# A 32-head attention with a gated GLU: the last two head groups alternate by chunk, output projections spread over the last blocks, |q| by a bit mask

## The chip, the cores and the metric

One core of a Trainium2 chip. Its engines work side by side, each on its own in-order stream of instructions: TensorE (PE, matmuls; the loads of its stationary operand are listed as PEld), VectorE (DVE), ScalarE (ACT), GpSimd (POOL) and SyncE (SP), which issues nearly all of the DMAs. The metric is the device time of one execution in microseconds; the median of the runs counts. A profile is one execution recorded by the hardware; its span runs from the first to the last instruction.

## The reference

With S = 2048 rows, D = 640, 32 heads of 20 channels and F = 1728:

```python
xn = layernorm(x)                                     # (2048, 640)
q, k, v = heads(xn @ wqkv)                            # 32 heads, Dh = 20
p = softmax(q @ k.T * Dh ** -0.5)                     # 2048 x 2048 for each head
s = concat_heads(p @ v) @ wo
g = silu((sigmoid(xn @ w_gate) * (xn @ w_up)) @ w_down)
out = x + s * g
```

All inputs and the output are bfloat16.

## The kernel before

**Blocks.** The heads are taken in 8 groups of 4 (`NG`, `GH`), the queries in 4 chunks of 512 (`NQC`, `QC`). A block is one group with one chunk, `g, c = divmod(b, NQC)`: 32 blocks, all four chunks of a group behind one another. A block has 4 x 16 score tiles of 128 keys x 512 queries. The four heads of a group lie 32 partitions apart, so that their small matmuls run beside each other in PE. The keys of a group are in `kTs[g % 2]`, the queries of a block in `qts[b % 3]`.

**Exponentials.** They are shared between two engines. ACT takes tiles in slots of two or three: two banks `scA[0]`/`scA[1]` of 128x1024, and at times one of the three spare banks `bank` (`bk` in the profile), with `exp_act` (L80). DVE takes the others from a `bk` bank: one conversion to int16 (`iv`, L1194) and, for four tiles at once, three passes (L945, L948, L951) that make two bfloat16 factors, which PE sums up; so a DVE tile costs two attention matmuls. The attention matmuls (L897) add into one bank, `oacc`, whose row 0 of each head is the sum of the exponentials.

**The quotient.** At a block's end `norm_a` copies `oacc` to `on` (L910) and sends the sums through DRAM (`ld`, `lt`); `norm_b` takes the reciprocal (`rt`), sends it through DRAM again (`rd`, `rl`), multiplies on POOL (`on_bf`, L927) and stores the heads' rows into `oU` (L935), the transposed input of the output projection, four or five DMAs for a block. For block 30, the last but one, another way is taken: `mk_div` transposes `on` on PE, divides on DVE, transposes back and keeps the group's 80 rows in `oL`; the projection of chunk 2 has a sixth matmul with `oL` and `wo_l`, the last 80 rows of `wo`. Block 31 takes the same way in the steps `e_on` (L985), `e_tr` (L989), `e_scale`, `e_back` (L998), `e_o` (L1002).

**The work around it.** Beside scores and attention, PE has items, each a list of operations on several engines in one spare bank: keys, queries and values of the next groups; for each chunk the GLU's gate and up (`mk_gu`, L641) and down (`mk_down`, L679; its `td` on ACT, `gqs` on DVE, then a store to `gq_dram`); and the output projection `mk_out` of a row tile `tt` and a half `h` of the columns. `mk_qu` makes the queries of 6 heads: an evacuation to `qu`, and |q| of it (L547), for a bound on the scores.

`mk_out(tt, h)` has five matmuls of 320 columns (L765), a `scalar_tensor_tensor` on DVE with the GLU result (`otmp`, L772), an addition of x on POOL or DVE (L775), and after the second half the store of the tile (L777). `load_out` brings x and the GLU result of the tile into one of three slots that lie over `xnT` (L743, L744); a slot is taken again by tile `tt + 3`.

**Tail.** The last chunk's four tiles are not made by `mk_out`. `fill` holds 40 early matmuls (L976): for each tile 5 of 512 and 5 of 128 columns over the rows of `oU` that the first seven groups fill. Those that the planner finds no gap for are put out at the start of `tail_steps`. Four plus four late matmuls (L980) add the last group, then come the evacuations (L1020 to L1032) and the stores (L1036). Their x and GLU rows are loaded by `tail_load` (L964, L965) into space of `wd`, the weights of the down projection, once no GLU item is left.

**Order.** PE, ACT and DVE run in an order written out by a planner in the kernel: a loop over a clock of its own, with a fixed cost for each operation, that decides at each step which engine takes what. PE fills an ACT slot when it is free and otherwise goes on with attention matmuls or an item. `items` have an earliest block (`at`), conditions (`pre`) and, for projections, a block whose quotient must be done (`need`); an item that may run goes ahead of the GLU's. `due()` says how much of the item work should be done by now; `M_END` is how many blocks before the end all of it should be. `can_fill` lets early matmuls in when all scores are claimed and PE has nothing else. SP and POOL are not planned: their streams follow the order in which buffers come free.

Of the kernel before, what the change touches and what calls it, by code (L numbers as in the profile page):

```python
# [10 lines left out]
FP32 = mybir.dt.float32  # L11
# [19 lines left out]
URGENT, ROUNDS, HOLD, SLACK, LEAD, LAG, D_LAST, D_LAST_END = 0.25, 4, 0.15, 0.2, 40.0, 0.0, 20, 8  # L31
D_ORD, M_ORD, WAIT3, FALL, M_END = 1, 0, 0.4, 1, 1.5
NPT, NPB, NIV = (3, 7), 3, 3
# [16 lines left out]
def kernel(  # L50
# [375 lines left out]

    NBLK = NG * NQC
    NJOB = GH * TT
    q_at = {0: 0.0}
# [109 lines left out]
    def mk_qu(u, c, at):  # L539
        st = {}  # L540

        def alloc():
            st["ps"] = misc_ps()

        def ab():
            aqs[(u, c)] = wk.tile([P, QC], BF16, tag="aq", bufs=4, name="aq")
            nc.vector.scalar_tensor_tensor(out=aqs[(u, c)][0:UC, :], in0=st["q"], scalar=-1.0, in1=st["q"],  # L547
                                           op0=ALU.mult, op1=ALU.max)

        def ev():  # L550
            st["q"] = wk.tile([P, QC], BF16, tag="ku", bufs=2, name="qu")[0:UC, :]
            nc.vector.tensor_scalar_mul(out=st["q"], in0=st["ps"][0:UC, :], scalar1=qscale)
            nc.sync.dma_start(out=qD[u][:, c * QC:(c + 1) * QC], in_=st["q"])
        return Item([("PE", alloc, [(T_MM, lambda kd=kd: u_mm(st, u, 0, c, kd)) for kd in range(KD)]),
                     ("DVE", 0.60, ev, "free", mark("qD", u, c)),
                     ("DVE", 0.60, ab, "", mark("aq", u, c))], at, pre=[("bD", u - 1)] if u else [])

# [38 lines left out]
    def load_q(b):  # L596
        g, c = divmod(b, NQC)
# [100 lines left out]
    wo_l = late.tile([GC, D], BF16, name="wo_l")  # L698
    oL = []

    def div_scale(tps):
# [6 lines left out]
        return onq  # L708

    def mk_div(on, b):  # L710
        st = {}

        def a1():
            st["t"] = misc_ps()

        def a2():
            st["u"] = misc_ps().bitcast(BF16)

        def tr(i):
            nc.tensor.transpose(out=st["t"][:, i * P:(i + 1) * P], in_=on[:, i * P:(i + 1) * P], identity=ident_f)  # L720

        def sc():
            st["q"] = div_scale(st["t"])

        def back():
            for i in range(4):
                nc.tensor.transpose(out=st["u"][0:GC, i * P:(i + 1) * P], in_=st["q"][:, i, :], identity=ident)

        def ev():
            o = w2.tile([GC, QC], BF16, tag="on_bf", bufs=2, name="oL")  # L730
            nc.vector.tensor_copy(out=o, in_=st["u"][0:GC, 0:QC])
            oL.append(o)
        return [Item([("PE", a1, [(0.22, lambda i=i: tr(i)) for i in range(4)]),
                      ("DVE", 0.75, sc, "free", mark("div", b))], 0.0, pre=[("on", b)]),
                Item([("PE", a2, [(0.30, back)]),
                      ("DVE", 0.40, ev, "free", lambda t: o_at.__setitem__(b, t))], 0.0, pre=[("div", b)])]

# [8 lines left out]
    def mk_out(tt, h, at):  # L746
        st = {}

        def alloc():
            if h == 0:  # L750
                load_out(tt)
                if (tt + 1) % 4:
                    load_out(tt + 1)
            st["ps"] = misc_ps()

        split = tt // 4 == NQC - 2

        def mm(kd):
            hs = slice(h * HD, (h + 1) * HD)
            if kd == KD:  # L760
                lhsT, rhs = oL[0][:, tt % 4 * P:(tt % 4 + 1) * P], wo_l[:, hs]
            else:
                rows = o_l if split and kd == t_l else P
                lhsT, rhs = oU[0:rows, kd, tt * P:(tt + 1) * P], wo[0:rows, kd, hs]
            nc.tensor.matmul(st["ps"][:, 0:HD], lhsT=lhsT, rhs=rhs, start=(kd == 0),  # L765
                             stop=(kd == KD - 1 + split))

        def ev():
            xr, gqr = out_tiles[tt]
            sl = slice(h * HD, (h + 1) * HD)  # L770
            tmp = w2.tile([P, HD], FP32, tag="gqs", bufs=3, name="otmp")
            nc.vector.scalar_tensor_tensor(out=tmp, in0=st["ps"][:, 0:HD], scalar=0.25,  # L772
                                           in1=gqr[:, sl], op0=ALU.mult, op1=ALU.mult)
            add = nc.vector if h == 1 and claimed[0] == NJOB * NBLK else nc.gpsimd
            add.tensor_tensor(out=xr[:, sl], in0=tmp, in1=xr[:, sl], op=ALU.add)  # L775
            if h == 1:
                nc.sync.dma_start(out=out2[tt * P:(tt + 1) * P, :], in_=xr)  # L777
        return Item([("PE", alloc, [(0.136, lambda kd=kd: mm(kd)) for kd in range(KD + split)]),
                     ("DVE", 0.40, ev, "free", mark("o", tt, h))], at, need=(NG - 1) * NQC + tt // 4,
                    pre=[("d", tt // 4, t4, i) for t4 in range(4) for i in range(2)] + [("h", 2, kf) for kf in range(NFT)] + (  # L780
                        [("o", tt - 2, 1)] if h == 0 and tt > 1 else []))
# [12 lines left out]
    for b in range(NBLK):  # L794
        g, c = divmod(b, NQC)
        mk = []
# [62 lines left out]
    def score_mm(dst, b, kt, j):  # L859
        nc.tensor.matmul(dst, lhsT=kTs[(b // NQC) % 2][32 * j:32 * j + 32, kt * P:(kt + 1) * P],  # L860
                         rhs=qts[b % 3][32 * j:32 * j + 32, :], start=True, stop=True, tile_position=(32 * j, 0))
# [16 lines left out]
    def pv_pick(j):  # L878
        for u in pv_q[j]:
            if u["b"] == pv_block[0] and u["ready"] <= now and v_at.get((u["b"] // NQC // 2, u["kt"]), 1e9) <= now:  # L880
                return u
        return None
# [4 lines left out]
    def pv_emit(us, end):  # L887
        for u in us:
            b, kt, j, k = u["b"], u["kt"], u["j"], u["k"]
            pr, go = divmod(b // NQC, 2)  # L890
            pv_q[j].remove(u)
# [25 lines left out]
    def norm_b(b, on, lt):  # L917
        g, c = divmod(b, NQC)
        rt = w2.tile([P, GH * QC // P], FP32, tag="rt", bufs=2, name="rt")
# [90 lines left out]
    def tail_steps():  # L1010
        for _, _, f in fill:
            f()
        for t4 in range(4):
# [24 lines left out]
    with tc.manual_schedule(engines={ENG.PE, ENG.Activation, ENG.DVE}):  # L1038
# [59 lines left out]
        chain_at = 1e9  # L1098
        while chain or items or glu_items or any(it.i < len(it.ops) for it in active):
            guard += 1  # L1100
            assert guard < 120000, "the issue order does not end"
            bb = base()
            if bb > blk_loaded:
                blk_loaded = bb
                g, c = divmod(bb, NQC)
                if c == 0 and g + 1 < PG:
# [18 lines left out]
            if q_next < NBLK and base() >= q_next - 2:  # L1125
                us_ = [u for u, _, _, _ in spans(q_next // NQC)]
                if all(ev_at.get(("qD", u, q_next % NQC), 1e9) <= now and ev_at.get(("bD", u), 1e9) <= now for u in us_) \
                        and q_next // NQC in k_at:
                    load_q(q_next)
                    q_at[q_next] = max(now + 5.0, k_at[q_next // NQC])  # L1130
                    q_next += 1

            for eng in ("ACT", "DVE"):
# [99 lines left out]
            if free["PE"] <= now:  # L1233
# [45 lines left out]
                if nxt == "F":  # L1279
# [111 lines left out]
```

## Time and profile before

| | us |
|---|---|
| runs (3) | 840.9, 841.19, 842.89 |
| median | 841.19 |
| profiled execution, span | 839.8 |
| mean granted TensorE clock | 0.997 |

A row of groups reads: line, engine, operation, out<-in, shapes, xcount | busy us, mean ns of one | idle time before them, and what ended it. A row of the timeline: start, length, engine, line, operation, xcount, and in brackets the idle time before it. A row of windows: stretch, its length, the busy time of each engine with its count of instructions, the granted clock, the share of the DMA engines, GB/s. The profile's line numbers are those of the kernel before.

### The profile page before, as it was taken

What the parts mean: (1) busy time and instruction counts of PE and PEld (TensorE: products, weight loads), DVE (VectorE), ACT (ScalarE), POOL (GpSimd) and SP (SyncE); (2) the same over time, 40 slices, a digit from 0 to 9 for tenths busy, and PEclk for the clock granted to TensorE, in tenths of its full rate; (3) what the DMA queues carried; (4) which work ended last, traced back from release to release, by engine and by line L of the source; (5) the groups of instructions that cost most, each with busy time, mean ns of one, the idle gap of its engine ahead of it and who ended that gap; (6) DMA issues with size and microseconds to landing.
All of it is one profiled execution on the core that took longest, in us unless ns stands there. A gap on an engine that the chain in (4) does not pass through costs nothing.

```text
span 839.8 us, 16932 instructions
## 1 busy us (share of the span) xinstructions
PE 788.4 (94%) x6354; PEld 278.5 (33%) x6411; DVE 765.4 (91%) x1194; ACT 796.0 (95%) x1003; POOL 77.5 (9%) x84
## 2 busy tenths in 40 slices
PE   4799999999999999999999999999999999999995
PEld 2432323333333323333333233333233322333342
DVE  7789899999899998998999999999998988999994
ACT  7799999999999999999999999999999999999970
POOL 5000000000000001000000000000000000002333
PEclk9999999999999999999999999999999999999998
DMA  5711212123222132213121232131311223111642
GB/s 154 205 51 50 60 51 49 47 57 82 72 62 63 43 85 69 68 44 82 52 61 53 68 85 67 45 92 49 109 65 46 66 71 78 28 47 57 193 147 91
DMA packets 92979, 62.21 MB, mean 74 GB/s; under 512 B 34648, under 2 KB 86408, under 8 KB 92896
## 3 DMA queue, kind: packets, MB, share of 16 engines
q1 hardware_dynamic: 92608, 60.79, 25.7%
q8 instruction: 50, 0.82, 0.4%
q10 hardware_dynamic: 288, 0.33, 0.1%
q14 instruction: 33, 0.27, 0.1%
HBM read 46.24 MB, written 12.39 MB: 70 GB/s over the span
## 4 chain that ended last, share of the span: by engine, by line
ACT 49%; PE 28%; DVE 13%; issue 6%; DMA 2%; SPq 1%; POOL 0%; POOLq 0%; ACTq 0%; DVEq 0%
ACT pt L80 44%; PE scA L860 8%; PE oacc L897 5%; DVE iv L1194 5%; PE bk L679 4%; PE bk L641 3%; ACT tnh L80 3%; DVE pb L951 2%; PE bk L765 2%; PE bk L504 2%; DVE pb L945 1%; DVE pb L948 1%; DMA ld<-on 1%; PE psk L140 1%; ACT td L80 1%
## 5 line engine op out<-in xcount | busy, mean ns | idle before, releaser
L80 ACT ACTIVATE pt<-scA 128x1024 bf16<-128x1024 f32 (+1 forms) x729 | 720.2, 1153 | 4.6 <-PE bk L860 2.9
L1194 DVE TENSOR_SCALAR iv<-bk 128x512 int16<-128x512 f32 x471 | 318.6, 682 | 31.7 <-PE bk L860 30.2
L860 PE MATMUL scA<-q,kT 32*128 32x512 bf16 x1448 | 282.6, 382 | 16.7 <-ACT pt L80 9.6
L860 PE MATMUL bk<-q,kT 32*128 32x512 bf16 x600 | 215.5, 383 | 2.0 <-DVE iv L1194 1.7
L897 PE MATMUL oacc<-pt,v 128*21 128x512 bf16 x1577 | 183.1, 382 | 0.6 <-ACT pt L80 0.3
L860 PEld LDWEIGHTS <-kT 32*128 32x128 bf16 x2048 | 88.7, 91 | 261.6 <-issue 246.8
L897 PE MATMUL oacc<-pb,v 128*21 128x512 bf16 x942 | 152.9, 382 | 1.8 <-DVE on L910 1.5
L951 DVE TENSOR_TENSOR pb<-iv,pb 128x2048 bf16<-128x2048 bf16 x118 | 146.8, 1244 | 0.8
L641 PE MATMUL bk<-xnT,wgu 128*128 128x512 bf16 x471 | 142.6, 383 | 3.6 <-issue 1.7
L927 POOL TENSOR_TENSOR on_bf<-on,rl 128x512 bf16<-128x512 f32 x30 | 43.3, 1443 | 692.7 <-DMA rl<-rd 326.0
L80 ACT ACTIVATE pt<-bk 128x512 bf16<-128x512 f32 x129 | 94.5, 733 | 4.0 <-PE bk L860 3.8
L945 DVE TENSOR_SCALAR pb<-iv 128x2048 int16<-128x2048 int16 x118 | 86.3, 731 | 2.5
L679 PE MATMUL bk<-wd,hT 128*128 128x320 bf16 x448 | 86.9, 302 | 1.2 <-DVE iv L1194 0.7
L948 DVE TENSOR_SCALAR pb<-iv 128x2048 int16<-128x2048 int16 x118 | 82.6, 700 | 0.0
L897 PEld LDWEIGHTS <-v 128*21 128x21 bf16 x2519 | 50.4, 90 | 92.2 <-issue 69.4
L641 PEld LDWEIGHTS <-wgu 128*128 128x128 bf16 x520 | 37.1, 97 | 66.2 <-issue 50.4
L679 PEld LDWEIGHTS <-hT 128*128 128x128 bf16 x448 | 34.4, 97 | 48.4 <-issue 39.4
L504 PE MATMUL bk<-xnT,wu 128*120 128x512 bf16 x160 | 49.3, 399 | 0.4 <-DVE iv L1194 0.3
L80 ACT ACTIVATE tnh<-bk 128x512 bf16<-128x512 f32 (+1 forms) x56 | 41.6, 742 | 0.1
L649 DVE SCALAR_TENSOR_TENSOR hT<-tnh,bk 128x512 bf16<-128x512 bf16 x52 | 35.3, 680 | 5.9 <-PE bk L641 5.2
L612 PE MATMUL bk<-wv,xnT 128*128 128x160 bf16 x280 | 29.2, 234 | 0.7 <-ACT pt L80 0.6
L612 PEld LDWEIGHTS <-xnT 128*128 128x128 bf16 x280 | 18.6, 98 | 14.4 <-issue 14.1
(116 smaller groups left out, 381.3 us busy)
## 6 DMA issues: line engine op xcount, KB each, us to landing
wgu<-in_B_w_gate_dram SPq DMA_DIRECT2D x24, 320.0 KB
wgu<-in_B_w_up_dram SPq DMA_DIRECT2D x24, 320.0 KB
rl<-rd SPq DMA_DIRECT2D x120, 64.0 KB
gq_dram<-gqs SPq DMA_DIRECT2D x32, 160.0 KB
xnT<-gq_dram SPq DMA_DIRECT2D x12, 320.0 KB
xt<-in_A_x_dram SPq DMA_DIRECT2D x16, 160.0 KB
wd<-in_B_w_down_dram SPq DMA_DIRECT2D x1, 2080.0 KB
oU<-on_bf SPq DMA_DIRECT2D x104, 20.0 KB
```

What stands on the lines that cost most here:

```text
L80: return nc.scalar.add_instruction(mybir.InstActivation(func=func, name=nc.get_next_instruction_name(), engine=ENG.Activation, ins=[nc.sca ...
L504: nc.tensor.matmul(st["ps"][0:UC, :], lhsT=wus[u][:, kd, i, :], rhs=xnT[:, c, kd, :], start=(kd == 0), stop=(kd == KD - 1))
L612: nc.tensor.matmul(st["ps"][:, i * 2 * GC:(i + 1) * 2 * GC], lhsT=xn_tok(tts[i], kd), rhs=wvs[pr][:, kd, :], start=(kd == 0), stop=(kd == ...
L641: nc.tensor.matmul(st[key][0:fs, :], lhsT=w[:, i, kd, ko * P:ko * P + fs], rhs=xnT[:, c, kd, :], start=(kd == 0), stop=(kd == KD - 1))
L679: nc.tensor.matmul(st["ps"][:, 0:HD], lhsT=hT[0:fsz[kf], kf, t4 * P:(t4 + 1) * P], rhs=wd[0:fsz[kf], kf, h * HD:(h + 1) * HD], start=(kf = ...
L860: nc.tensor.matmul(dst, lhsT=kTs[(b // NQC) % 2][32 * j:32 * j + 32, kt * P:(kt + 1) * P], rhs=qts[b % 3][32 * j:32 * j + 32, :], start=Tr ...
L897: nc.tensor.matmul(oacc[32 * j:32 * j + DH + 1, :], lhsT=lhsT, rhs=u["src"], start=first, stop=last, tile_position=(0, 32 * j), skip_group ...
L927: nc.gpsimd.tensor_tensor(out=on_bf, in0=on, in1=rl, op=ALU.mult)
L945: nc.vector.tensor_scalar(out=pb[:, 0, :, :].bitcast(I16), in0=iv, scalar1=0x7F80, scalar2=1, op0=ALU.bitwise_and, op1=ALU.bitwise_or)
L948: nc.vector.tensor_scalar(out=pb[:, 1, :, :].bitcast(I16), in0=iv, scalar1=0x007F, scalar2=0x3F00, op0=ALU.bitwise_and, op1=ALU.bitwise_or)
L951: nc.vector.tensor_tensor(out=pb[:, 1, :, :], in0=iv.bitcast(BF16), in1=pb[:, 1, :, :], op=ALU.mult)
L1194: nc.vector.tensor_scalar(out=d["iv"][:, j, :], in0=bank[bk], scalar1=B_OFF, scalar2=0.0, op0=ALU.add, op1=ALU.max)
```

## The change

1. From block 24 (`ALT`) on, groups 6 and 7 alternate: block 24 is group 6 chunk 0, block 25 group 7 chunk 0, block 26 group 6 chunk 1, and so on. The keys of both groups stay in their two buffers. A chunk's attention is complete after blocks 25, 27, 29 and 31, where before it was after 28, 29, 30 and 31.
2. The projections are listed four halves to a block from block 26 on, with `need` at the chunk's own last block.
3. Block 30 takes the quotient's common way; `mk_div`, `oL` and the sixth matmul are gone. Block 30 is now group 6, chunk 3.
4. The early matmuls that were left to `tail_steps` are all given out in the planner's loop, which goes on until they are.
5. |q| is made by clearing the sign bit of the bfloat16 value as an int16, planned at 0.19 in place of 0.60 us.
6. `M_END` goes from 1.5 to 2.25 blocks.

```diff
-D_ORD, M_ORD, WAIT3, FALL, M_END = 1, 0, 0.4, 1, 1.5
+D_ORD, M_ORD, WAIT3, FALL, M_END = 1, 0, 0.4, 1, 2.25
...
+    ALT = (NG - 2) * NQC
+
+    def gc_of(b):
+        if b < ALT:
+            return divmod(b, NQC)
+        return NG - 2 + (b - ALT) % 2, (b - ALT) // 2
...
-            nc.vector.scalar_tensor_tensor(out=aqs[(u, c)][0:UC, :], in0=st["q"], scalar=-1.0, in1=st["q"],
-                                           op0=ALU.mult, op1=ALU.max)
+            nc.vector.tensor_scalar(out=aqs[(u, c)][0:UC, :].bitcast(I16), in0=st["q"].bitcast(I16), scalar1=0x7FFF,
+                                    scalar2=0, op0=ALU.bitwise_and, op1=ALU.bitwise_or)
...
-                     ("DVE", 0.60, ab, "", mark("aq", u, c))], at, pre=[("bD", u - 1)] if u else [])
+                     ("DVE", 0.19, ab, "", mark("aq", u, c))], at, pre=[("bD", u - 1)] if u else [])
...
-    def mk_div(on, b):
...
-        split = tt // 4 == NQC - 2
-
         def mm(kd):
             hs = slice(h * HD, (h + 1) * HD)
-            if kd == KD:
-                lhsT, rhs = oL[0][:, tt % 4 * P:(tt % 4 + 1) * P], wo_l[:, hs]
-            else:
-                rows = o_l if split and kd == t_l else P
-                lhsT, rhs = oU[0:rows, kd, tt * P:(tt + 1) * P], wo[0:rows, kd, hs]
-            nc.tensor.matmul(st["ps"][:, 0:HD], lhsT=lhsT, rhs=rhs, start=(kd == 0),
-                             stop=(kd == KD - 1 + split))
+            nc.tensor.matmul(st["ps"][:, 0:HD], lhsT=oU[:, kd, tt * P:(tt + 1) * P], rhs=wo[:, kd, hs],
+                             start=(kd == 0), stop=(kd == KD - 1))
...
-        return Item([("PE", alloc, [(0.136, lambda kd=kd: mm(kd)) for kd in range(KD + split)]),
-                     ("DVE", 0.40, ev, "free", mark("o", tt, h))], at, need=(NG - 1) * NQC + tt // 4,
+        return Item([("PE", alloc, [(0.136, lambda kd=kd: mm(kd)) for kd in range(KD)]),
+                     ("DVE", 0.40, ev, "free", mark("o", tt, h))], at, need=ALT + 1 + 2 * (tt // 4),
...
-        if b >= NBLK - NQC and c > 0:
-            for t4 in range(4):
-                for h in range(2):
-                    mk.append(lambda at, t=4 * (c - 1) + t4, h=h: [mk_out(t, h, at)])
+        if b >= ALT + 2:
+            n = (b - ALT - 2) * 4
+            for i in range(n, n + 4):
+                mk.append(lambda at, t=i // 2, h=i % 2: [mk_out(t, h, at)])
...
     def tail_steps():
-        for _, _, f in fill:
-            f()
...
-        while chain or items or glu_items or any(it.i < len(it.ops) for it in active):
+        while chain or fill or items or glu_items or any(it.i < len(it.ops) for it in active):
...
-                    if norm_pending[0] == NBLK - 2:
-                        on = w2.tile([P, QC], FP32, tag="on", bufs=2, name="on")
-                        nc.vector.tensor_copy(out=on, in_=oacc)
-                        items[0:0] = mk_div(on, norm_pending[0])
-                        ev_at[("on", norm_pending[0])] = free["DVE"] + EL
-                    else:
-                        timed.append((free["DVE"] + 6.5, norm_pending[0]) + norm_a(norm_pending[0]))
+                    timed.append((free["DVE"] + 6.5, norm_pending[0]) + norm_a(norm_pending[0]))
...
-                    elif m_ok:
-                        nxt = "M"
+                    else:
+                        nxt = "M" if m_ok else None
```

Elsewhere `divmod(b, NQC)` and `b // NQC` become `gc_of(b)`, in the loads of keys and queries, the scores, the values and the quotient.

More of the change, by code (lines that the diff above doesn't have):

```diff
@@ L596, in load_q @@
     def load_q(b):
-        g, c = divmod(b, NQC)
+        g, c = gc_of(b)
         cs = slice(c * QC, (c + 1) * QC)
@@ L698 @@
     wo_l = late.tile([GC, D], BF16, name="wo_l")
-    oL = []
     def div_scale(tps):
@@ L708, in div_scale @@
         return onq
-    def mk_div(on, b):
[L711 to L736, printed above, removed]
     def load_out(tt):
@@ L794 @@
     for b in range(NBLK):
-        g, c = divmod(b, NQC)
+        g, c = gc_of(b)
         mk = []
@@ L859, in score_mm @@
     def score_mm(dst, b, kt, j):
-        nc.tensor.matmul(dst, lhsT=kTs[(b // NQC) % 2][32 * j:32 * j + 32, kt * P:(kt + 1) * P],
+        nc.tensor.matmul(dst, lhsT=kTs[gc_of(b)[0] % 2][32 * j:32 * j + 32, kt * P:(kt + 1) * P],
                          rhs=qts[b % 3][32 * j:32 * j + 32, :], start=True, stop=True, tile_position=(32 * j, 0))
@@ L879, in pv_pick @@
         for u in pv_q[j]:
-            if u["b"] == pv_block[0] and u["ready"] <= now and v_at.get((u["b"] // NQC // 2, u["kt"]), 1e9) <= now:
+            if u["b"] == pv_block[0] and u["ready"] <= now and v_at.get((gc_of(u["b"])[0] // 2, u["kt"]), 1e9) <= now:
                 return u
@@ L889, in pv_emit @@
             b, kt, j, k = u["b"], u["kt"], u["j"], u["k"]
-            pr, go = divmod(b // NQC, 2)
+            pr, go = divmod(gc_of(b)[0], 2)
             pv_q[j].remove(u)
@@ L917, in norm_b @@
     def norm_b(b, on, lt):
-        g, c = divmod(b, NQC)
+        g, c = gc_of(b)
         rt = w2.tile([P, GH * QC // P], FP32, tag="rt", bufs=2, name="rt")
@@ L1104 @@
                 blk_loaded = bb
-                g, c = divmod(bb, NQC)
+                g, c = gc_of(bb)
                 if c == 0 and g + 1 < PG:
@@ L1125 @@
             if q_next < NBLK and base() >= q_next - 2:
-                us_ = [u for u, _, _, _ in spans(q_next // NQC)]
-                if all(ev_at.get(("qD", u, q_next % NQC), 1e9) <= now and ev_at.get(("bD", u), 1e9) <= now for u in us_) \
-                        and q_next // NQC in k_at:
+                us_ = [u for u, _, _, _ in spans(gc_of(q_next)[0])]
+                if all(ev_at.get(("qD", u, gc_of(q_next)[1]), 1e9) <= now and ev_at.get(("bD", u), 1e9) <= now for u in us_) \
+                        and gc_of(q_next)[0] in k_at:
                     load_q(q_next)
-                    q_at[q_next] = max(now + 5.0, k_at[q_next // NQC])
+                    q_at[q_next] = max(now + 5.0, k_at[gc_of(q_next)[0]])
                     q_next += 1
```

## The prediction

> **What bounds the kernel now.** I read the page's engine totals and slices first, then the busy time by stage, then the end of the run in order of time.
>
> ```profile
> span 839.8 us, 16932 instructions
> PE 788.4 (94%) x6354; PEld 278.5 (33%) x6411; DVE 765.4 (91%) x1194; ACT 796.0 (95%) x1003; POOL 77.5 (9%) x84
> PE   4799999999999999999999999999999999999995
> ACT  7799999999999999999999999999999999999970
> ```
>
> ScalarE (ACT) is full from the third slice to the last but one, and then empty while TensorE (PE) goes on. The stages, with the busy time of each engine:
>
> ```profile
> core 0: us, PE busy (x) PEld busy (x) DVE busy (x) ACT busy (x) POOL busy (x), PEclk, DMA share, GB/s
> 60.00:812.70 752.70, 727.06 (x5889) 249.04 (x5939) 705.23 (x1074) 746.51 (x921) 56.22 (x45) 1.00 0.24 68
> 777.00:787.00 10.00, 9.84 (x84) 3.58 (x82) 9.93 (x17) 10.00 (x12) 4.79 (x6) 1.00 0.52 160
> 812.70:823.00 10.30, 10.28 (x67) 5.14 (x65) 8.14 (x17) 0.00 (x0) 2.67 (x4) 1.00 0.55 175
> 823.00:830.30 7.30, 7.27 (x44) 3.10 (x44) 1.07 (x3) 0.00 (x0) 1.41 (x2) 1.00 0.20 67
> 830.30:839.80 9.50, 0.87 (x5) 0.20 (x2) 4.94 (x7) 0.00 (x0) 3.82 (x3) 0.73 0.20 71
> ```
>
> From 60 us to 812.7 ACT is idle for 752.70 - 746.51 = 6.2 us, VectorE (DVE) for 47.5, PE for 25.6: the exponentials set the pace. From 812.7 on ACT has nothing; PE is the bound for 17.6 us, and the last 9.5 us are the final evacuations and stores. So the time is the end of the last exponential, E, plus a tail.
>
> ```profile
> 799.64 6.53 ACT L80 ACTIVATE pt<-scA 128x1024 bf16<-128x1024 f32 x7
> 805.97 0.70 ACT L80 ACTIVATE pt<-bk 128x512 bf16<-128x512 f32 x1
> 806.45 2.06 ACT L80 ACTIVATE pt<-scA 128x1024 bf16<-128x1024 f32 x2
> 808.73 3.96 ACT L80 ACTIVATE pt<-scA 128x1024 bf16<-128x1024 f32 x4
> ```
>
> E = 808.73 + 3.96 = 812.69, and the tail is 839.8 - 812.69 = 27.1 us. From start to start a 128x1024 exponential costs (805.97 - 799.64) / 7 = 0.904 us and a 128x512 one 806.45 - 805.97 = 0.48; the longer means below overlap.
>
> **The change, part by part.** The issue orders of the two built programs (they hold no times) give the counts.
>
> *Exponentials.* The planner hands six score tiles more to ACT: 728 exponentials of 128x1024 in place of 719, 127 of 128x512 in place of 139 (129 + 10 below).
>
> ```profile
> L80 ACT ACTIVATE pt<-scA 128x1024 bf16<-128x1024 f32 x719 | 715.3, 1160 | 4.6 <-PE bk L860 2.9 <-PE scA L860 1.0
> L80 ACT ACTIVATE pt<-bk 128x512 bf16<-128x512 f32 x129 | 94.5, 733 | 4.0 <-PE bk L860 3.8
> L80 ACT ACTIVATE td<-bk 128x320 bf16<-128x320 f32 x32 | 17.3, 541 | 0.0
> L80 ACT ACTIVATE pt<-scA 128x512 bf16<-128x512 f32 x10 | 7.1, 708 | 0.0
> ```
>
> That is 9 x 0.904 - 12 x 0.48 = +2.4 us on the engine that sets the pace. One `td` now stands behind the last exponential; it takes about 0.4 us out from in front of E. If ACT's idle time stays as it is, E' = 812.69 + 2.4 - 0.4 = 814.7. The idle time is the unknown: at best its 6.2 us vanish, at worst I allow as much again.
>
> *Bit mask.* Sixteen instructions of 703 ns change form. No bitwise row has 512 elements; those of 1536 and 2048 carried on in a straight line give 551 - 2 x 150 = 251 ns and 546 - 2 x 187 = 172 ns, and 551 is an upper bound. I take 0.21.
>
> ```profile
> L945 DVE TENSOR_SCALAR pb<-iv 128x2048 int16<-128x2048 int16 x117 | 85.8, 733 | 2.5
> L948 DVE TENSOR_SCALAR pb<-iv 128x2048 int16<-128x2048 int16 x117 | 82.0, 701 | 0.0
> L547 DVE SCALAR_TENSOR_TENSOR aq<-qu 120x512 bf16<-120x512 bf16 x16 | 11.3, 703 | 0.0
> L948 DVE TENSOR_SCALAR pb<-iv 128x1536 int16<-128x1536 int16 x1 | 0.6, 551 | 0.0
> L945 DVE TENSOR_SCALAR pb<-iv 128x1536 int16<-128x1536 int16 x1 | 0.5, 546 | 0.0
> ```
>
> DVE is freed of 16 x 0.49 = 7.9 us (2.4 at the upper bound). On the path this is worth nothing: DVE already has 47.5 us idle beside a full ACT, and the score tiles move the other way. It would count only if DVE's lateness made ACT's 6.2 us of idle time.
>
> *Projections out of the tail.* Before, some 50 output matmuls stand on PE after E. After, all 120 stand ahead of the last score, and the eight with `oL` are gone with the two transposes of `mk_div`. Five `wd` matmuls and the 40 early matmuls remain after the last score. Prices:
>
> ```profile
> 808.29 0.84 PE L765 MATMUL bk<-wo,oU 128*128 128x320 bf16 x5 [0.23 <-DVE iv L1194]
> 814.72 0.68 DVE L985 COPY on<-oacc 128x512 f32<-128x512 f32 x1
> 815.46 0.66 PE L989 MATMUL scA<-ident_f,on 128*128 128x128 f32 x4
> 817.46 0.39 PE L998 MATMUL tp<-ident,onq 128*80 128x128 bf16 x4
> 823.03 2.42 PE L976 MATMUL scA<-wo,oU 128*128 128x512 bf16 x9
> 825.38 4.60 PE L976 MATMUL bk<-wo,oU 128*128 128x512 bf16 x30
> 830.34 0.69 DVE L1020 SCALAR_TENSOR_TENSOR hT<-bk,wd 128x512 f32<-128x512 f32 x1 [5.02 <-PE bk L980]
> ```
>
> 50 x 0.84 / 5 = 8.4 us of PE work goes under ACT, where PE has 25.6 us idle; I cost it at nothing, and at up to 8.4 us if that room is not usable. The added quotient chain of block 30 (one POOL multiplication, five kinds of DMA) lies beside the last block.
>
> Tail before: 2.0 us from E to the copy of `oacc` (814.72), 15.6 us to the first evacuation (830.34), 9.5 us to the end. The last stays. Of the twenty 512-wide early matmuls (0.245 us each: ten in 2.42), seven now stand between the last attention matmuls, thirteen behind the copy, then the twenty 128-wide ones (4.60 less ten at 0.25, so 2.1 us). From the copy to the first evacuation: 13 x 0.245 + 0.66 + 0.39 + 2.1, and 0.36 for the late ones (825.38 + 4.60 to 830.34), = 6.7 us. From E' to the copy I take 2.9 instead of 2.0, since four of the seven stand ahead of the last attention matmul. PE is then ready at E' + 9.6.
>
> *What is late next.* Two transfers. The early matmuls read block 30's `oU`, where before block 27's was the last they needed; and the reload of the GLU result for the tail, hidden before, now begins when the last `wd` matmul has run, because it overwrites `wd`.
>
> ```profile
> 770.93 0.68 DVE L910 COPY on<-oacc 128x512 f32<-128x512 f32 x1
> ```
>
> ```profile
> 785.91 3.04 SPq L935 DMA_DIRECT2D oU<-on_bf  x4
> 789.05 0.42 SPq L777 DMA_DIRECT2D out_dram<-xnT  x1
> 789.52 0.92 SPq L964 DMA_DIRECT2D wd<-in_A_x_dram  x1
> 794.33 0.38 SPq L691 DMA_DIRECT2D gq_dram<-gqs  x1
> 799.90 0.32 SPq L965 DMA_DIRECT2D wd<-gq_dram  x1
> ```
>
> Copy to last `oU` issue was 788.95 - 770.93 = 18.0 us; with a fifth `oU` transfer (0.76) and about 2 us to land, 21. Block 30's copy stands 18 score fills before the end: 18 x 0.904 + 5 x 0.48 + some 1.1 = 19.8 us before E'. So `oU` lands near E' + 1.2; the matmul that reads it is due at E' + 1.4 to 1.7. It just fits, within about 2 us either way.
>
> Before, nine loads (five of 160 KB, four of 320) and the store at 794.33 (160 KB) took from 789.52 until 799.90, when the load that waits for that store went out: 2240 KB in 10.4 us. SP's queue is in order, so after, the first load goes out at about E' + 0.2, behind block 30's `oU` and tile 11's store; six loads (1440 KB) stand before the last store (160 KB). 1600 / 2240 x 10.4 = 7.4 us, so the last reload goes out at E' + 7.6 and lands some 2.9 later (2.4 as in the row among the rivals, and the doubled size): E' + 10.5. That is later than PE's E' + 9.6, so the transfer decides, by 0.9.
>
> The Trainium skill, "DMA: Bandwidth & Descriptors", section Bandwidth, measures 341 GB/s for 1 MB, which as an estimate moves 1600 KB in 4.8 us; PE would decide then and the sum would be 0.9 lower. The row is of the same loads in the same company, and I keep it.
>
> Sum: 814.7 + 10.5 + 9.5 = 834.7 us of span. The profiled execution's span is 839.8 and the runs' median 841.19; with the same 1.4 us around it, **836 us**.
>
> **Rivals.**
> - *The tail's transfers are later still* (0.13). For it: no matmul waited for these `oU` rows before, and the quotient chain now shares SP's queue with the stores of tiles 8 to 10, each waiting for its POOL addition. Against: both were priced with company. 3.5 us more: 839.5.
> - *PE has no room* (0.10). The 8.4 us come back, less what ACT absorbs, as a later E: about 842, no change. For it: only 25.6 us of 752.7 idle. Against: from 800 to E projections ran beside exponentials standing start to start. The Trainium skill, "Trace Analysis", section Identifying the Most-Contended Engine, says that matmul busy time is a bad measure of PE's headroom and weight-load time a better one; here that is 249.04 of 752.7. By the page there is ample room and this rival would be worth 0.05; the sum is the same by both.
> - *Slower: the tiles' turnover holds DVE* (0.08). Three slots in `xnT` serve twelve tiles. A slot takes its next row of x only when the last store has landed, and DVE's in-order `otmp` stands before the int16 conversions whose banks PE needs:
>
> ```profile
> 778.39 2.39 DMA out_dram<-xnT
> 780.80 2.20 DMA xnT<-in_A_x_dram
> ```
>
> Two such pieces in a row are 4.6 us, against some 1.8 us of exponentials queued ahead. It decides from 0.65 us lost per tile (7.8 in twelve); at 1 us each, 848. Against: while this very chain ran, ACT was busy 10.00 of 10.00 us (777 to 787), and the tiles are now spread over five blocks in place of three.
> - *DVE was the hidden bound* (0.05): the mask's 7.9 us let ACT's idle time nearly vanish: 831.
>
> **How the numbers follow.** The forecast has 0.64, spread over 832 to 838.7 by the idle time (about 3 either way) and the transfers (about 2). The range from 831 to 843.5 leaves out the slower rival and the ends of the others, some 0.14. Counting as equal what lies within 0.3% of 841.19 (838.7 to 843.7): faster 0.72 (forecast 0.62, hidden bound 0.05, late tail 0.05), same 0.16, slower 0.12.
>
> **What would show it.** Right: the last exponential ends at 813 to 817; no output projection after it; the copy of `oacc` 2.5 to 3.5 us later; the first evacuation some 10.5 us after E', waiting for a transfer of `wd<-gq_dram` rather than for PE; the bit mask near 0.2 us, and DVE idler than before. Wrong: E' beyond 820 with ACT idle in front of score matmuls, PE waiting for `oU` before its early matmuls for over 3 us, or `otmp` waiting for transfers in the last eight blocks.

## The result and the profile after

| | before | after |
|---|---|---|
| median, us | 841.4 (4 runs, 840.9 to 842.89) | 837.4 (4 runs, 835.54 to 838.14) |
| ratio of the times, 95% interval | | 0.9947 [0.9932, 0.9961] |
| profiled execution: time, span | span 839.8 | 838.14, span 836.4 |
| end of the last exponential, E | 812.69 | 816.77 |
| E to the copy of `oacc` | 2.0 | 3.05 |
| E to the first evacuation | 17.65 | 10.64 |
| E to the end (tail) | 27.1 | 19.6 |

The change makes the kernel faster by 0.5%. The page of after, its first lines and two rows of its slices:

```profile
span 836.4 us, 16903 instructions
PE 782.4 (94%) x6330; PEld 276.5 (33%) x6389; DVE 751.7 (90%) x1178; ACT 798.5 (95%) x1000; POOL 83.2 (10%) x90
PE   4899999999999999999999999999999999999995
ACT  7699999999999999999999999999999999999990
```

The totals of PE and ACT hardly move, DVE's falls by 13.7 us. ACT's last busy slice is fuller (9 in place of 7), and the whole run ends earlier. The end of ACT's stream in after, from its timeline:

```profile
815.20 0.66 ACT L80 ACTIVATE pt<-bk 128x512 bf16<-128x512 f32 x1
815.67 1.10 ACT L80 ACTIVATE pt<-scA 128x1024 bf16<-128x1024 f32 x1
816.58 0.53 ACT L80 ACTIVATE td<-bk 128x320 bf16<-128x320 f32 x1
```

E' (the E of after) = 815.67 + 1.10 = 816.77, 4.1 us later than before. After it stands one `td`, as the issue order said. The tail of after, in the timelines of PE and DVE:

```profile
817.37 0.59 PE L946 MATMUL scA<-wo,oU 128*128 128x512 bf16 x2 [0.16 <-issue]
818.22 1.25 PE L946 MATMUL scA<-wo,oU 128*128 128x512 bf16 x4
819.40 0.39 PE L867 MATMUL oacc<-pb,v 128*21 128x512 bf16 x1
822.96 2.87 PE L946 MATMUL bk<-wo,oU 128*128 128x512 bf16 x23
825.76 0.40 PE L950 MATMUL bk<-wo_l,o 80*128 80x128 bf16 x4
```

```profile
819.82 0.69 DVE L955 COPY on<-oacc 128x512 f32<-128x512 f32 x1 [1.79 <-PE oacc L867]
827.41 0.69 DVE L988 SCALAR_TENSOR_TENSOR hT<-bk,wd 128x512 f32<-128x512 f32 x1 [3.77 <-DMA wd<-gq_dram]
```

No output projection (L735) stands behind E'. The 0.16 us before the first early matmul are no wait for block 30's `oU`: the same 0.16 us stand there with M_END 1.5 (below), where the early matmuls begin 7.5 us after E. So no wait for the quotient's transfers shows; by how much they were in time isn't shown. PE is ready for the first evacuation at 825.76 + 0.40, which is E' + 9.4. The reload of the last GLU tile comes last: DVE, idle for 3.77 us, goes on 1.25 us after PE is ready. The chain of waits of after and SP's queue:

```profile
820.11 4.44 DMA gq_dram<-gqs
...
824.62 2.72 DMA wd<-gq_dram
...
827.41 0.70 DVE hT L988
```

```profile
816.89 0.37 SPq L934 DMA_DIRECT2D wd<-in_A_x_dram  x1
...
820.11 0.33 SPq L697 DMA_DIRECT2D gq_dram<-gqs  x1
820.54 0.98 SPq L934 DMA_DIRECT2D wd<-in_A_x_dram  x1
824.62 0.32 SPq L935 DMA_DIRECT2D wd<-gq_dram  x1
```

The loads begin 0.1 us after E', the store stands behind six of them, and the reload goes out when the store has landed, 824.62 - 816.89 = 7.7 us after the first load (7.4 forecast).

Half of the reason why E' is late lies in the head of the run. Two stretches of after, then the same of before; the columns are stretch and length, busy time of PE, PEld, DVE, ACT, POOL, the granted clock, the DMA share and GB/s:

```profile
31.00:35.00 4.00, 1.53 (x10) 0.33 (x9) 3.01 (x7) 1.21 (x4) 0.00 (x0) 0.80 1.13 315
35.00:40.50 5.50, 5.49 (x38) 3.43 (x38) 2.35 (x4) 4.32 (x5) 0.00 (x0) 0.52 1.07 362
```

```profile
31.00:35.00 4.00, 1.81 (x18) 0.99 (x19) 3.02 (x7) 1.46 (x3) 0.00 (x0) 1.00 1.13 308
35.00:40.50 5.50, 4.96 (x52) 2.71 (x51) 4.29 (x7) 5.50 (x8) 0.00 (x0) 1.00 1.08 350
```

In both, PE has just waited 1.30 and 0.79 us for DVE. In the profile of after the granted clock then goes to 0.52, PE is full and yet feeds ACT 4.32 us of work in place of 5.50. Over the first 60 us ACT is busy 47.47 us in after and 49.48 in before: 2.0 us, half of E's delay. This is not the change. The kernel with doubled output matmuls, below, has after's issue order there and keeps 1.00; the run with the mask alone has the order of before and falls to 0.50. Their second stretches, in this order:

```profile
35.00:40.50 5.50, 5.03 (x53) 2.70 (x53) 4.46 (x8) 5.50 (x7) 0.00 (x0) 1.00 1.08 350
35.00:40.50 5.50, 5.50 (x35) 3.04 (x33) 3.33 (x6) 4.53 (x6) 0.00 (x0) 0.50 1.09 344
```

The fastest of the four runs of after, 835.54 us, had a mean clock of 0.996; the others took 836.98 to 838.14 us at 0.990 to 0.992. The other half of E's delay is work, the longer list of exponentials: from 60 us to E' ACT is idle for 756.77 - 750.69 = 6.1 us, as before (6.2).

```profile
60.00:816.77 756.77, 729.08 (x5928) 250.37 (x5980) 699.54 (x1072) 750.69 (x920) 66.19 (x55) 1.00 0.25 68
```

### The profile page after: what moved, and what is told of

Its sections match the earlier page's. It is cut to its first block, busy times and chain, and to the rows that moved or that the text cites. A ratio compares the mean times of both kernels' runs of the same rounds, so it can differ in the third digit from the quotient of the medians.

```text
span 836.4 us, 16903 instructions
## 1 busy us (share of the span) xinstructions
PE 782.4 (94%) x6330; PEld 276.5 (33%) x6389; DVE 751.7 (90%) x1178; ACT 798.5 (95%) x1000; POOL 83.2 (10%) x90
## 4 chain that ended last, share of the span: by engine, by line
ACT 49%; PE 29%; DVE 11%; issue 7%; DMA 2%; SPq 1%; POOLq 0%; POOL 0%; ACTq 0%; DVEq 0%
ACT pt L80 45%; PE scA L830 9%; PE oacc L867 6%; PE bk L685 4%; DVE iv L1156 4%; PE bk L647 4%; ACT tnh L80 2%; DVE pb L921 2%; PE bk L510 2%; DVE pb L915 1%; DVE pb L918 1%; PE bk L735 1%; PE bk L618 1%; PE psk L140 1%; DMA lt<-ld 1%
## 5 line engine op out<-in xcount | busy, mean ns | idle before, releaser
L80 ACT ACTIVATE pt<-scA 128x1024 bf16<-128x1024 f32 x734 | 722.1, 1147 | 5.7 <-PE bk L830 1.9
L830 PE MATMUL scA<-q,kT 32*128 32x512 bf16 x1462 | 285.8, 384 | 17.9 <-ACT pt L80 10.5
L830 PE MATMUL bk<-q,kT 32*128 32x512 bf16 x586 | 211.7, 386 | 1.4 <-DVE iv L1156 1.2
L867 PE MATMUL oacc<-pb,v 128*21 128x512 bf16 x930 | 150.6, 382 | 1.0 <-DVE pb L915 0.4
L921 DVE TENSOR_TENSOR pb<-iv,pb 128x2048 bf16<-128x2048 bf16 (+1 forms) x117 | 145.6, 1245 | 0.7
L80 ACT ACTIVATE pt<-bk 128x512 bf16<-128x512 f32 x121 | 86.7, 717 | 4.2 <-DVE oacc L388 2.8
L915 DVE TENSOR_SCALAR pb<-iv 128x2048 int16<-128x2048 int16 (+1 forms) x117 | 84.5, 722 | 2.7
L918 DVE TENSOR_SCALAR pb<-iv 128x2048 int16<-128x2048 int16 (+1 forms) x117 | 83.4, 713 | 0.0
L618 PE MATMUL bk<-wv,xnT 128*128 128x160 bf16 x280 | 31.6, 243 | 1.1 <-DVE v L189 0.5
L745 POOL TENSOR_TENSOR xnT<-otmp,xnT 128x320 bf16<-128x320 f32 x24 | 24.2, 1011 | 45.7 <-DVE otmp L742 45.5
```

The lines of the kernel that those rows point to most:

```text
L80: return nc.scalar.add_instruction(mybir.InstActivation(func=func, name=nc.get_next_instruction_name(), engine=ENG.Activation, ins=[nc.sca ...
L618: nc.tensor.matmul(st["ps"][:, i * 2 * GC:(i + 1) * 2 * GC], lhsT=xn_tok(tts[i], kd), rhs=wvs[pr][:, kd, :], start=(kd == 0), stop=(kd == ...
L830: nc.tensor.matmul(dst, lhsT=kTs[gc_of(b)[0] % 2][32 * j:32 * j + 32, kt * P:(kt + 1) * P], rhs=qts[b % 3][32 * j:32 * j + 32, :], start=T ...
L867: nc.tensor.matmul(oacc[32 * j:32 * j + DH + 1, :], lhsT=lhsT, rhs=u["src"], start=first, stop=last, tile_position=(0, 32 * j), skip_group ...
L915: nc.vector.tensor_scalar(out=pb[:, 0, :, :].bitcast(I16), in0=iv, scalar1=0x7F80, scalar2=1, op0=ALU.bitwise_and, op1=ALU.bitwise_or)
L918: nc.vector.tensor_scalar(out=pb[:, 1, :, :].bitcast(I16), in0=iv, scalar1=0x007F, scalar2=0x3F00, op0=ALU.bitwise_and, op1=ALU.bitwise_or)
```

## The experiments

The ratio is always to the kernel before, run beside it on the same chip. "ACT idle" is ACT's idle time between 60 us and E in the profiled execution (before 6.2, after 6.1).

**The mask alone.** Before, with only the |q| instruction exchanged; its planned cost stays 0.60, so the order is that of before.

```diff
-            nc.vector.scalar_tensor_tensor(out=aqs[(u, c)][0:UC, :], in0=st["q"], scalar=-1.0, in1=st["q"],
-                                           op0=ALU.mult, op1=ALU.max)
+            nc.vector.tensor_scalar(out=aqs[(u, c)][0:UC, :].bitcast(I16), in0=st["q"].bitcast(I16), scalar1=0x7FFF,
+                                    scalar2=0, op0=ALU.bitwise_and, op1=ALU.bitwise_or)
```

> The kernel before with the bit mask alone; the planner's cost for it stays 0.60, so the issue order is the one of before and only 16 DVE instructions get shorter (703 to 280 ns each, 6.8 us together). Theory (ACT sets the pace and DVE has spare time beside it): no change, 841.4 within 0.8. Rival (DVE was the hidden bound): the 6.8 us come out, 834 to 836.

Measured: 842.15 us, ratio 0.9997 [0.9981, 1.0013], ACT idle 5.2. In this order the mask is worth nothing. (E is 2.0 us later than in the profile of before; that arises in the head, where its clock was at 0.50.)

**The old |q| in after's order.** The reverse exchange in after, planned cost still 0.19.

> The changed kernel with the old |q| instruction (703 ns) in the changed issue order, so DVE gets 6.8 us more work and nothing moves. Theory (the mask gave nothing): 837.4 within 0.8. Rival (the mask gave the gain): 841 to 844.

Measured: 841.73 us, 1.0012 [0.9991, 1.0032]; the whole gain is gone. E is 820.76, ACT idle 10.6. The groups of |q| in after, and in this run:

```profile
L553 DVE TENSOR_SCALAR aq<-qu 120x512 int16<-120x512 int16 x16 | 4.5, 280 | 0.0
```

```profile
L553 DVE SCALAR_TENSOR_TENSOR aq<-qu 120x512 bf16<-120x512 bf16 x16 | 10.9, 679 | 0.0
```

So 6.4 us more of DVE work make E 4.0 us later, although DVE is idle for 57 us between 60 us and E in after, and for 56 in this run:

```profile
60.00:820.76 760.76, 730.84 (x5921) 249.91 (x5974) 704.75 (x1071) 750.15 (x918) 67.69 (x55) 1.00 0.24 68
```

The order of both is the same, so each ACT instruction can be set beside its like. At 60 us this run is 1.5 us ahead of after, whose clock fell further in the head, so it loses 5.5 us from there on; the ratios differ by 0.65%, as much. Of this 1.3, 1.2 and 2.5 us are lost where the second, third and fourth of the four groups of |q| stand, none at the first. Another 1.5 us is lost near 215 us, far from any |q| (see the last section), and 1.0 is won back elsewhere. At the last group, in windows of this run:

```profile
572.00:574.00 2.00, 1.06 (x13) 0.48 (x9) 2.00 (x4) 1.70 (x2) 0.11 (x1) 1.00 0.20 73
574.00:576.00 2.00, 2.00 (x18) 0.38 (x15) 2.00 (x4) 1.02 (x1) 0.00 (x0) 0.57 0.11 29
576.00:578.00 2.00, 2.00 (x15) 0.99 (x12) 1.96 (x3) 1.75 (x2) 0.00 (x0) 0.58 0.05 14
```

DVE is full, PE waits for it (1.06 of 2.00 us busy), and for the next 4 us the granted clock is near a half and ACT starves.

**M_END back to 1.5**, in after (`M_END` 2.25 to 1.5).

> The changed kernel with M_END back at 1.5. The planner then hands out 719 exponentials of 128x1024 and 141 of 128x512 (1.4 us less on ACT than with 2.25), but 38 down matmuls instead of 5 stand behind the last score, so the tail's loads into wd start 33 x 0.17 = 5.6 us later. Theory (end = last exponential + a tail that the last down matmul, its store and the reload set): about 837.4 - 1.4 + 4.6 = 840.6, the first tail evacuation still waiting for wd<-gq_dram. Rival (the number of exponentials alone sets the time): 836.

Measured: 837.86 us, 0.9956 [0.9941, 0.9972]; no difference from after that can be told, where 840.6 was expected. The tail is longer by 6.1 us (25.7), and E is earlier by 4.5 (812.3), not by the 1.4 that the counts of exponentials gave: with 1.5, 38 down-projection matmuls are left behind the last score. Most of what M_END takes out of the tail comes back before E.

**M_END at 4.0**, in after.

> The changed kernel with M_END 4.0. The planner hands out 730 exponentials of 128x1024 and 115 of 128x512 (4.0 us less on ACT), and the last down matmul stands 196 scores before the end, so the tail's reload is over long before it is needed. Theory: 837.4 - 4.0 - 1.1 = 832.3, the last exponential at about 813, the first tail evacuation about 9.6 us after it and released by PE. Rival (item work taken earlier keeps PE from the scores, and ACT idles more than 6 us between 60 us and its end): 837 or more.

Measured: 852.23 us, 1.0138 [1.0108, 1.0169], a miss by 20 us. The tail is 18.1, but E is 832.72 and ACT idle 24.9, as the rival had it. Its ACT group and two windows:

```profile
L80 ACT ACTIVATE pt<-scA 128x1024 bf16<-128x1024 f32 x730 | 716.5, 1124 | 20.9 <-PE bk L830 9.9 <-PE scA L830 5.0 <-PE oacc L867 4.7
```

```profile
746.00:750.00 4.00, 2.17 (x11) 0.68 (x9) 1.48 (x4) 2.69 (x3) 0.00 (x0) 0.89 0.09 19
750.00:755.00 5.00, 5.00 (x31) 0.99 (x29) 2.79 (x5) 2.38 (x3) 1.27 (x1) 0.50 0.46 151
```

Here a reciprocal of the quotient stood in DVE's stream 3.54 us ahead of the DMA that it reads; PE paused 1.80 us behind it, and the clock halved for 5 us. These two windows hold 3.9 of the 18.8 us that ACT idles more than in after; the rest is spread over the run (8.0 us are idle from 500 to 600 us, 2.0 in after), and its causes stay open.

**Reload on ACT's queue.** After, with the last store of the GLU and the load that waits for it issued by ACT.

```diff
-            nc.sync.dma_start(out=gq_dram[tt * P:(tt + 1) * P, h * HD:(h + 1) * HD], in_=gqs)
+            eng = nc.scalar if tt == TT - 1 and h == 1 else nc.sync
+            eng.dma_start(out=gq_dram[tt * P:(tt + 1) * P, h * HD:(h + 1) * HD], in_=gqs)
...
-            nc.sync.dma_start(out=tail[t4][1], in_=gq_dram[r, :])
+            (nc.scalar if t4 == 3 else nc.sync).dma_start(out=tail[t4][1], in_=gq_dram[r, :])
```

> The changed kernel with the last GLU store and the reload that depends on it issued from ACT's DMA queue in place of SP's; the order on PE, DVE and POOL stays. Theory (the store is late because it is queued behind the six loads into wd, 1440 KB, on SP's ring): the store lands about 2.2 us after its issue instead of 4.4, the reload about 4 us earlier than in the changed kernel, and the first tail evacuation is released by PE, 1.1 us earlier: 836.3. Rival (all queues share the same DMA engines, so the store waits behind the same packets): no change, 837.4.

Measured: 835.58 us, 0.9931 [0.9916, 0.9945], the lowest median of all, though the interval overlaps that of after, so the times alone don't tell the two apart. The chain of waits of this run:

```profile
817.43 5.21 DMA gq_dram<-gqs
...
822.79 3.29 DMA wd<-gq_dram
...
826.17 0.70 DVE hT L989
```

The store goes out 2.7 us earlier and takes 0.8 longer, the load 0.6 longer; the evacuation comes at E + 9.69 in place of 10.64. So the gain is the earlier issue; the store did not land sooner after it, as had been expected (2.2 us). The transfer did decide the tail, and it still comes last: PE is ready at E + 9.4 as in after, 0.3 us ahead of the evacuation, so little more is to be had there.

**Output matmuls doubled.** After, with the five output matmuls of each item issued twice over, 120 more in all, the planner not told. The second five start the sum anew and repeat the work.

```diff
+            for kd in (2 * list(range(KD)))[2 * step:2 * step + 2]:
+                nc.tensor.matmul(st["ps"][:, 0:HD], lhsT=oU[:, kd, tt * P:(tt + 1) * P], rhs=wo[:, kd, hs],
+                                 start=(kd == 0), stop=(kd == KD - 1))
```

> The changed kernel with each of the 120 output matmuls issued twice (the first set of five is overwritten by the second), the planner not told: 20.4 us more PE work at 0.17 us each between 690 us and the last score, where PE shows 4.2 us idle. Theory by matmul busy time (PE has hardly any room there): the last exponential some 12 to 16 us later, 850 to 853. Rival (PE's busy time overstates how full it is, weight loads fill 33% of it): 838 to 841.

Measured: 850.04 us, 1.0121 [1.0094, 1.0148]. The order is the same as in after, so the stretch can be taken from the same exponential on, one that stands ahead of all the output matmuls: 690.92 us in after, 687.90 in this run, whose clock did not fall in the head. From there to E, in after and in this run:

```profile
690.92:816.77 125.85, 121.67 (x1028) 43.02 (x1031) 118.51 (x183) 125.16 (x156) 32.28 (x30) 1.00 0.28 82
```

```profile
687.90:825.83 137.93, 135.95 (x1148) 53.34 (x1151) 119.88 (x183) 128.24 (x156) 32.28 (x30) 1.00 0.26 76
```

The 120 more matmuls add 14.3 us to PE's busy time, not the 20.4 reckoned, and 12.1 us to the stretch. Only 2.2 us of them go into after's 4.2 us of PE idle time.

**No alternation.** Before, with the mask (planned 0.19), M_END 2.25 and the early matmuls in the loop, but the old order of blocks and the old places of the projections.

> The kernel before with everything of the change but the alternation and the projections' new places: bit mask at 0.19, M_END 2.25, early matmuls in the planner's loop. 728 exponentials of 128x1024 and 125 of 128x512 (1.4 us more on ACT than before), and 73 projection and early matmuls in spare banks behind the last score as before (75). Theory (the gain is the shorter tail, and that is the alternation's): 841 to 843, the tail from the last exponential to the end still 26 to 28 us. Rival (the planner's parameters and the rest give the gain): 837 to 838.

Measured: 848.79 us, 1.0087 [1.0065, 1.0108], where 841 to 843 was expected. Tail 26.6, ACT idle 10.0. Windows and a PE row of this run:

```profile
764.00:769.00 5.00, 3.31 (x36) 0.80 (x24) 3.80 (x7) 5.00 (x8) 0.00 (x0) 0.92 0.35 120
769.00:778.00 9.00, 8.89 (x54) 2.10 (x56) 7.98 (x13) 7.81 (x10) 1.26 (x1) 0.50 0.22 66
```

```profile
768.57 0.58 PE L860 MATMUL scA<-q,kT 32*128 32x512 bf16 x1 [0.69 <-ACT pt L80]
```

This is the reverse of too much work: with the GLU done early and the projections not yet allowed, PE has nothing beside scores and attention from 763 us, the last down matmul, to 775.9, the first output matmul; it waits for ACT, 0.70 and 0.69 us within 2.1 us. Then the clock is at 0.50 for 9 us, and PE, which was waiting, cannot keep up. This is one part of the loss: from 763 to 780 us ACT is idle for 1.9 of its 10.0 us. Between 60 and 700 us it idles 5.7 us (3.1 in the run with M_END 1.5 below), and why stays open.

**The mask planned at 0.60**, and **the old |q| planned at 0.60**, both in after and with the same issue order.

```diff
-                     ("DVE", 0.19, ab, "", mark("aq", u, c))], at, pre=[("bD", u - 1)] if u else [])
+                     ("DVE", 0.60, ab, "", mark("aq", u, c))], at, pre=[("bD", u - 1)] if u else [])
```

> The changed kernel with the bit mask, but planned at 0.60 us as the old instruction was. The issue order is new: 721 exponentials of 128x1024, 140 of 128x512 (0.1 us less on ACT), eight down matmuls behind the last score instead of five. Theory (an instruction that is done earlier than planned is worth nothing, one that is done later costs its lateness): the order was planned without the mask's gain, and the alternation carries it, 837.5 to 838.5. Rival (the gain comes from planning with the short mask): 840 to 842.

> The same issue order as e8, with the old |q| instruction (about 690 ns, planned at 0.60). Theory (only lateness against the plan costs): at most 16 x 0.09 = 1.4 us more than e8, 838 to 839.5; then the alternation without any mask keeps most of the gain. Rival (the instruction's whole length is on the path in the blocks where it stands, as in e2): 16 x 0.40 = 6.4 us more than e8, 843 to 845.

Measured: 837.97 us, 0.9949 [0.9927, 0.997], and 839.15 us, 0.9949 [0.993, 0.9968]. With an order that was planned for 0.60, the slow instruction costs nothing that can be told (1.2 us by the medians, none by the ratios). E is no later with it either (815.11 against 815.66 with the mask). So what the old |q| costs depends on the order, and with M_END at 2.25 the alternation gains without the mask. That the cost is the time beyond the plan fits all these runs; with two orders compared it is argued, not shown.

**Reload on ACT's queue with M_END 2.4.**

> A candidate: e5 (last GLU store and its reload on ACT's DMA queue) with M_END 2.4 instead of 2.25. The planner hands out 729 exponentials of 128x1024 and 122 of 128x512 (1.5 us less on ACT), the last down matmul stands 66 scores before the end (so its td, its store and the reload are all hidden), all projections ahead of the last score, nine attention matmuls behind it instead of 23. Theory: 835.6 - 1.5 - 0.4 - up to 1 = 832.7 to 834. Rival (item work taken earlier makes ACT idle more, as in e4): 836 or more.

Measured: 846.71 us, 1.0045 [1.0026, 1.0065]; E 828.49, ACT idle 16.5. The number was as the rival had it, but the run doesn't test it cleanly: with this order the last GLU store stands 66 score matmuls ahead of the end, and the moved transfers block ACT. Its timeline and windows:

```profile
796.31 0.34 ACTq L698 DMA_DIRECT2D gq_dram<-gqs  x1
800.62 0.33 ACTq L936 DMA_DIRECT2D wd<-gq_dram  x1
801.05 2.85 ACT L80 ACTIVATE pt<-scA 128x1024 bf16<-128x1024 f32 x3 [4.61 <-DMA gq_dram<-gqs]
```

```profile
796.00:802.00 6.00, 1.05 (x8) 0.49 (x7) 2.47 (x5) 1.39 (x3) 0.79 (x1) 0.74 0.61 190
802.00:811.00 9.00, 8.88 (x48) 2.06 (x47) 5.81 (x9) 6.90 (x8) 1.58 (x2) 0.50 0.26 88
```

The load waits for the store at the head of ACT's queue and every exponential behind it waits too, 4.61 us; PE stops, and the clock is at a half for the 9 us that follow, in which ACT loses 2.1 more. The rival has its part as well: from 60 to 796 us, ahead of all this, ACT is idle for 8.8 us, more than the 6.1 of after up to E.

**Old order of blocks with M_END 1.5**, and **the alternation alone**: the first is the run without alternation with 1.5 in place of 2.25, the second is after with the old |q| at 0.60 and M_END 1.5.

> The kernel of the run without alternation (848.8 us), with M_END back at 1.5; so this is before with the bit mask planned at 0.19 and the early matmuls given out in the loop. Theory (M_END at 2.25 cost that run its time: item work is drawn forward into blocks where PE has no room): back at 841 to 843, ACT idle 5 to 7 us between 60 us and the last exponential, tail about 27 us. Rival (the new issue order that the cheaper planned mask brings is at fault): 846 or more, ACT idle 9 us or more.

> The alternation with the new places of the projections and the early matmuls given out in the loop, alone: old |q| instruction planned at 0.60, M_END 1.5. Theory (the alternation carries the gain, and mask and M_END add nothing that can be measured): 837 to 839.5, ratio to before 0.994 to 0.998, with a tail near 25.7 us as in the run with M_END 1.5 and a last exponential near 812 to 814. Rival (it needs M_END at 2.25, since with 1.5 the down projections that are left fill the tail): 840.5 or more, tail 27 us or more.

Measured: 841.88 us, 1.0005 [0.9992, 1.0019], ACT idle 4.3, tail 29.5 (27 was expected); and 840.87 us, 0.9995 [0.9979, 1.0011], ACT idle 4.8, tail 25.9. The first settles that M_END at 2.25, not the mask's place in the plan, cost the run without alternation its 7 us. The second is a miss: alone, the alternation gains nothing that can be told. In its tail stand 22 down matmuls in one row, where the output projections used to be:

```profile
816.82 0.84 PE L685 MATMUL bk<-wd,hT 128*128 128x320 bf16 x5
817.50 0.39 PE L968 MATMUL tp<-ident,onq 128*80 128x128 bf16 x4
817.72 3.46 PE L685 MATMUL bk<-wd,hT 128*128 128x320 bf16 x22
```

That alone is not why: with the mask and M_END 1.5, which gains, 16 stand in this place, and the tail, 25.7 us, is as long.

All together, the ratios (the two measured kernels of the old order with the mask also give out the early matmuls in the loop):

| | old order of blocks | alternation |
|---|---|---|
| old \|q\| at 0.60, M_END 1.5 | 1 | 0.9995 |
| old \|q\| at 0.60, M_END 2.25 | not run | 0.9949 |
| mask at 0.19, M_END 1.5 | 1.0005 | 0.9956 |
| mask at 0.19, M_END 2.25 | 1.0087 | 0.9947 (after) |

No part that was run by itself gains; M_END alone was not run. The alternation with either the mask or M_END has the whole gain, and the third part adds nothing that can be told.

## Why the prediction was right, point by point

- **The exponentials.** 728 and 127, as counted. ACT's idle time from 60 us to E was 6.1 us against the 6.2 kept. E' was forecast at 814.7 and came at 816.77; the 2.0 us are those of the first 60 us. The step took ACT's idle time as given, from one profile, and that of before was one whose clock did not fall in the head. The forecast of 836 fits the one run of after with a mean clock like that profile's (0.996): 835.54 us.
- **The bit mask.** The price, 0.21 us, measured 0.280, inside the bounds. "On the path this is worth nothing" holds in before's order (0.9997) and, for M_END 2.25, for mask and plan together (0.9947 with them, 0.9949 without). The reason given for it failed. In after's order the old instruction costs about 5 us, with DVE idle for 56: the idle time that the argument pointed to lies in other blocks than the |q|. With M_END 1.5 mask and plan together are worth 0.4% (0.9995 to 0.9956). That nothing was lost by the wrong reason is luck: the sum needed the two only together.
- **50 output matmuls at no cost.** Right for this change as a sum (ACT's idle time did not grow), but not because the room was free: PE's idle time between 60 us and E, 25.6 us, became 27.7. The run with doubled matmuls lost 12.1 us of E to 14.3 us of PE work, and M_END 1.5 gives 4.5 us of E back for 6.1 of tail. The Trainium skill, "Perfetto Trace Analysis", section Identifying the Most-Contended Engine, would have had ample room by the weight loads (43.02 of 125.85 us); by the doubled run the matmul busy time, 121.67 of 125.85, was the better guide here. The rival without room was nearer than its 0.10.
- **The tail.** Copy at E' + 3.05 (forecast 2.9), PE ready at E' + 9.4 (9.6), first evacuation at E' + 10.64 (10.5), waiting for `wd<-gq_dram`, and 9.0 to the end (9.5). No wait for `oU` shows. That the transfer decides by about 1 us is shown by the trace (1.25 us after PE) and by the reload on ACT's queue (0.95 us less). The price from rows of before (7.4 us for 1600 KB) held; the faster one would have had PE decide.
- **The sum.** 814.7 + 10.5 + 9.5 = 834.7 against 816.77 + 10.64 + 8.99 = 836.4. The profiled run was the slowest of its four; the median, 837.4, is 1.4 above the forecast of 836.
- **The rivals.** The slots' turnover did not hold DVE: from 690 us to E no `otmp` waits for a transfer in after, and three wait 1.4 us in all for PE. DVE as the hidden bound falls with the mask alone. Later transfers in the tail did not occur.

What stays open: why alternation with M_END 1.5 gains with the mask (0.9956) and not with the old |q| (0.9995). The two profiles differ by 1.3 us of span, the medians by 3.0. The clock goes with it: the nine runs with the mask have a mean granted clock of 0.994 on average, the twelve with the old |q| 0.991, and the one of these at 0.996 took 837.74 us. Why the clock falls more often in that order is open too.

## What to carry to other kernels

Idle time of an engine summed over the run says little where the order is fixed: price an instruction against what the plan allows for it in its own block, and check that the plan's cost is the measured one. Work moved off a tail needs a place where the pacing engine's feeder has room at that moment, with neither too much (it starves the pacing engine) nor too little beside it (it pauses). And a transfer that waits for another one belongs on no queue whose engine still has work behind it.

## What the runs showed of the hardware

The granted clock of TensorE fell to 0.50 after pauses of PE, and stayed there for 5 to 9 us although PE was busy nearly all that time: after 3.31 busy of 5.00 us (769 to 778 in the run without alternation), 2.17 of 4.00 (M_END 4.0), 1.05 of 6.00 (M_END 2.4). Score matmuls in that time took 0.60 us in place of 0.39. The Trainium skill, "TensorE: Matmul & The Clock Gate", section Why this matters for your kernels, warns of gaps above about 3 us. The third case, a wait of 4.73 us, is one. In the others no single wait was longer than 0.70 and 1.80 us, so shorter ones are enough, and the measurement decides.

The same pause doesn't always do it. The old |q| in after's order has the instructions of after, and in both runs PE waits 1.10 us for ACT at the same place, 35 us behind the first group of |q|. In after, and then in that run:

```profile
213.36 0.39 PE L830 MATMUL scA<-q,kT 32*128 32x512 bf16 x2 [1.10 <-ACT pt L80]
213.91 0.39 PE L867 MATMUL oacc<-pt,v 128*21 128x512 bf16 x3
```

```profile
211.94 0.39 PE L830 MATMUL scA<-q,kT 32*128 32x512 bf16 x2 [1.10 <-ACT pt L80]
212.50 0.64 PE L867 MATMUL oacc<-pt,v 128*21 128x512 bf16 x3
```

After's clock stays at 1.00; that of the other run is at 0.53 from 214 to 216 us, and ACT loses 1.5 us. The head is a second case: the same two waits, 1.30 and 0.79 us, left the clock at 1.00 in before and were followed by 0.52 in after. What decides between the two outcomes, no run here shows. The 78 runs of before that ran beside the experiments show what goes with it: the 29 with a mean clock of 0.995 or more have a median of 840.67 us, the 49 others 842.53.
